# Transposes by DMA, permuted q/k weights, paired score rounds and a due-time order in a kernel of two attention and two FFN layers

## The chip, the cores and the metric

The kernel runs on one core of one Trainium2 chip. The metric is the device time of one execution in microseconds. The core's engines are TensorE (PE, with its weight loads as PEld), VectorE (DVE), ScalarE (ACT), GpSimd (POOL) and SyncE (SP, which here only issues DMAs). Each runs its own instruction list in order, and they meet at semaphores.

## The reference

x has 2048 tokens of 640 features. The program is x = x + A(LN(x)); x = x + B(LN(x)), done twice with the same weights. All inputs are bf16.

```python
def A(x):                     # 32 heads of 20, 4 segments of 512 tokens
    q, k, v = heads(x @ wq), heads(x @ wk), heads(x @ wv)
    M, z = 0, 0
    for s in range(4):
        p = softmax(q_s @ k_s.T * 20**-0.5 + causal_mask)
        a_dot = p @ v_s
        a_mem = (phi(q_s) @ M) / (phi(q_s) @ z + 1e-6)
        o_s = g * a_mem + (1 - g) * a_dot         # g = sigmoid(beta), per head
        M, z = M + phi(k_s).T @ v_s, z + phi(k_s).sum()
    return concat(o) @ wo
# phi(t) = t + 1 if t > 0 else exp(t)
def B(x): return relu(x @ w1) @ w2                # 640 -> 1728 -> 640
```

## The kernel before

The work goes by layer a (0, 1) and segment s (0 to 3) of 512 tokens, four tiles of 128 tokens each. The whole of x stays in SBUF as `x_sb`. Generators (streams) yield operations; the class `Sched` takes at each step the operation that can start earliest by planned durations, and among equals the one of the stream with the smaller priority number. It does so while the program is built: what comes out is a fixed list of instructions for each engine. The streams are, from the first priority on, `scores`, `apply`, `repack`, `memory`, `proj`, `ffn`, then the constants and the loads.

`proj` (per segment) normalises: `stats` takes mean and variance of each tile on DVE (L419, L421), `chain` computes 1/sqrt in nine small DVE operations for the four tiles together (L429 to L436), then each tile is scaled (L465), transposed by five TensorE matmuls against `ident` into a PSUM bank (L444) and copied out to `xnT` (L448 on DVE or L449 on ACT). Then k and q come feature-major in five chunks of 128 features, each from five matmuls of 512 columns (L497), and are copied to `stg`; V comes token-major, in halves of 320 columns (L516), into `v_aug`, which holds a 21st column of ones per head.

A head has 20 features, so the chunks of 128 cut heads in two. `repack` therefore moves k and q by DMAs on SP's queue (L547) from `stg` to `pad`, where four heads (a group) stand at partitions 0, 32, 64 and 96.

`scores` takes one item, that is one group g of one segment: four heads run in four row tiles of TensorE, in three rounds: key block 0 (512 columns), blocks 1 and 3 (384 + 128), block 2 (256) (L695). Each round fills PSUM tiles X and Y, from which ACT takes the exponential to `PT` (L702), and POOL masks the diagonal blocks (L709). `apply` multiplies `PT` by `v_aug` (40 matmuls of 21 columns, L730), and DVE divides, weights by 1 - g and, for s > 0, adds to what `memory` has written in `o_sb`.

`memory` makes phi(q) and multiplies by the block-diagonal `BD` (L588), writes the quotient to `o_sb` (L600), transposes k back to tokens on TensorE (L622), makes phi(k), and adds phi(k).T v to `M_sb` (L649 to L659). `o_sb` has two buffers, one for each parity of s; `memory` takes it only when the output projection of two segments before has read it.

`ffn` is one stream: `out_proj` (transposes of `o_sb` through L444, then ten matmuls of 320 columns per tile, L786, added to x at L764), the second normalisation, 70 matmuls of 512 columns (L807) with ReLU to `hT` (L813, L811), and 112 of 320 columns (L826), added to x. The next segment's `out_proj` starts after the last of these. PSUM has eight banks: four for X and Y, one for `apply`, and three (MISC) for all else.

## Time and profile before

| | |
|---|---|
| median of 3 runs | 796.89 us (796.12 to 797.0) |
| span of the profiled execution | 797.5 us |
| mean granted TensorE clock | 0.902 |
| busy: PE, DVE, ACT, POOL | 84%, 54%, 54%, 22% |
| HBM read, written | 10.33 MB, 2.62 MB |

An engine's busy time is the union of its instructions' intervals. The idle time before an instruction is given with the instruction that released it. Matmuls overlap, so the cost of one in a stream is read from the distance between starts or from a long run of them, and not from its own duration.

### The profile page before, as it was taken

How to read it: one execution, taken by the hardware profiler on the slowest of the kernel's cores; microseconds unless marked ns; L12 is line 12 of the kernel's file. 1: busy time of each engine (PE TensorE's matmuls, PEld its weight loads, DVE VectorE, ACT ScalarE, POOL GpSimd, SP SyncE). 2: the span in 40 equal slices, each digit the busy share in tenths (PEclk: the TensorE clock that was granted, in tenths of full speed). 3: DMA queues.
4: the chain of work that ended last, by engine and by line, in shares of the span. 5: the costliest groups of instructions: out<-in, count | busy, mean ns of one | idle time of the engine just before them, and what ended most of it. 6: DMA issues, size and time to landing. Idle time of an engine off the chain costs nothing.

```text
span 797.5 us, 16459 instructions
## 1 busy us (share of the span) xinstructions
PE 667.2 (84%) x6944; PEld 383.1 (48%) x6944; DVE 433.7 (54%) x1253; ACT 430.1 (54%) x593; POOL 172.3 (22%) x274
## 2 busy tenths in 40 slices
PE   0969579999987999889995899859998599579488
PEld 0435345546554455555463545635556346336335
DVE  4333769697378533783449745496453833611611
ACT  0467778887885686478821678216781175021030
POOL 3022333333332223122310233103330032000000
PEclk9969759999997999979997799967999699969889
DMA  8711100200110110002000020000200000000000
GB/s 283 261 42 32 37 1 9 46 16 2 41 28 1 36 33 2 1 8 46 18 1 1 6 47 17 1 1 10 46 14 35 1 1 18 18 0 25 9 0 34
DMA packets 22809, 24.50 MB, mean 31 GB/s; under 512 B 3472, under 2 KB 22096, under 8 KB 22736
## 3 DMA queue, kind: packets, MB, share of 16 engines
q1 hardware_dynamic: 22592, 23.44, 10.9%
q8 instruction: 54, 0.88, 0.4%
q14 instruction: 19, 0.16, 0.1%
q0 software_dynamic: 144, 0.02, 0.0%
HBM read 10.33 MB, written 2.62 MB: 16 GB/s over the span
## 4 chain that ended last, share of the span: by engine, by line
PE 73%; DVE 20%; ACT 4%; issue 1%; DMA 1%; POOLq 0%
PE ps L807 16%; PE ps L826 16%; PE ps L497 12%; PE ps L730 7%; PE ps L695 7%; PE ps L516 6%; DVE stats L419 5%; PE ps L786 4%; ACT PT L702 3%; PE ps L444 3%; DVE x_sb L764 3%; DVE xnT L448 2%; DVE xn_tok L465 2%; DVE o_sb L600 2%; PE ps L649 1%
## 5 line engine op out<-in xcount | busy, mean ns | idle before, releaser
L702 ACT ACTIVATE PT<-ps 128x1024 bf16<-128x1024 f32 (+1 forms) x384 | 317.5, 880 | 133.0 <-PE ps L695 131.9
L709 POOL TENSOR_SCALAR_AFFINE_SELECT PT<-PT 128x512 bf16<-128x512 bf16 x256 | 165.9, 660 | 492.2 <-ACT PT L702 492.1
L807 PE MATMUL ps<-xnT,w_r 128*128 128x512 bf16 x560 | 145.6, 391 | 2.2 <-DVE xnT L448 1.8
L764 DVE TENSOR_TENSOR x_sb<-x_sb,ps 128x320 bf16<-128x320 bf16 x128 | 61.9, 484 | 144.4 <-PE ps L826 128.1
L826 PE MATMUL ps<-w_r,hT 128*128 128x320 bf16 x896 | 131.4, 299 | 3.7 <-ACT hT L813 2.9
L826 PEld LDWEIGHTS ps<-w_r,hT 128*128 128x128 bf16 x896 | 84.5, 98 | 42.6 <-issue 5.9
L695 PE MATMUL ps<-pad 20*128 20x512 bf16 (+3 forms) x1024 | 75.3, 328 | 17.2 <-ACT PT L702 16.8
L813 ACT ACTIVATE hT<-ps 128x512 bf16<-128x512 f32 x62 | 37.1, 598 | 97.0 <-PE ps L807 96.6
L730 PEld LDWEIGHTS ps<-v_aug,PT 128*128 128x128 bf16 x2560 | 74.0, 98 | 23.3 <-issue 12.3
L730 PE MATMUL ps<-v_aug,PT 128*128 128x21 bf16 x2560 | 76.0, 174 | 9.6 <-DVE rstd L436 4.5
L444 PE MATMUL ps<-ident,xn_tok 128*128 128x128 bf16 x320 | 36.8, 262 | 56.2 <-DVE xn_tok L465 55.9
L807 PEld LDWEIGHTS ps<-xnT,w_r 128*128 128x128 bf16 x560 | 51.9, 100 | 60.6 <-issue 11.6
L786 PE MATMUL ps<-wo_r,oT 128*128 128x320 bf16 x320 | 53.2, 308 | 20.4 <-DVE oT L448 12.7
L497 PE MATMUL ps<-xnT,wk_r 128*128 128x512 bf16 x200 | 58.2, 407 | 1.0 <-DVE xnT L448 0.6
L695 PEld LDWEIGHTS ps<-pad 20*128 20x128 bf16 x1024 | 20.9, 93 | 78.0 <-ACT PT L702 43.0
L444 PEld LDWEIGHTS ps<-ident,xn_tok 128*128 128x128 bf16 x320 | 24.6, 116 | 70.2 <-DVE xn_tok L465 66.6
L497 PE MATMUL ps<-xnT,wq_r 128*128 128x512 bf16 x200 | 56.8, 396 | 0.0
L419 DVE BATCH_NORM_STATS2 stats<-x_sb 128x6 f32<-128x320 bf16 x128 | 55.6, 461 | 0.0
L516 PE MATMUL ps<-wv_r,xnT 128*128 128x320 bf16 x320 | 55.3, 300 | 0.2 <-DVE xnT L448 0.2
L811 DVE TENSOR_SCALAR hT<-ps 128x512 bf16<-128x512 f32 x50 | 34.4, 689 | 35.2 <-PE ps L807 34.8
L739 DVE RECIPROCAL rden<-ps 128x16 f32<-128x16 f32 x64 | 16.3, 255 | 60.9 <-PE ps L730 60.7
L786 PEld LDWEIGHTS ps<-wo_r,oT 128*128 128x128 bf16 x320 | 28.7, 99 | 35.9 <-DVE oT L448 16.0
(63 smaller groups left out, 578.5 us busy)
## 6 DMA issues: line engine op xcount, KB each, us to landing
pad<-stg SPq DMA_DIRECT2D x224, 40.0 KB
out_dram<-x_sb SPq DMA_DIRECT2D x16, 160.0 KB, 1.8
w_r<-in_B_w_dram SPq DMA_DIRECT2D x1, 2160.0 KB, 14.8
w_r<-in_B_w_dram SPq DMA_DIRECT2D x1, 2080.0 KB, 16.2
x_sb<-in_A_x_dram SPq DMA_DIRECT2D x3, 640.0 KB, 12.5
wk_r<-in_A_wk_dram SPq DMA_DIRECT2D x1, 800.0 KB, 9.1
wq_r<-in_A_wq_dram SPq DMA_DIRECT2D x1, 800.0 KB, 10.9
wv_r<-in_A_wv_dram SPq DMA_DIRECT2D x1, 800.0 KB, 12.6
```

Source lines behind the costliest of these rows:

```text
L419: tk = yield dve(320, 1, lambda e, c2=c2: e.bn_stats(stats6[:, t, c2, :], x_sb[:, t, c2 * 320:(c2 + 1) * 320]), xt)
L444: tk = yield pe(56.0 * FC, [(lambda e, c=c: e.transpose(pb[:, c * 128:(c + 1) * 128], srcs[c], ident[:]), c == FC - 1) for c in range(FC)] ...
L497: tk = yield pe(mm_ns(512), [(lambda e, k=k, w_r=w_r, c=c, bk=bk: e.matmul(bk.ap[:, :], w_r[:, k, c * 128:(c + 1) * 128], xt.ap[:, k, :], ...
L516: tk = yield pe(mm_ns(320), [(lambda e, k=k, i=i, hf=hf, bk=bk: e.matmul(bk.ap[:, 0:320], xt.ap[:, k, i * 128:(i + 1) * 128], wv_r[:, k, h ...
L695: fns.append((lambda e, j=j, hh=hh, N=N, o=o: e.matmul(ps[:, hh, o:o + N], sl.ap[32 * hh:32 * hh + DH, 0, 128 * j:128 * j + 128], sl.ap[32 ...
L702: tx = yield act(2 * w, lambda e, k=k, bkp=bkp, u=u, w=w: e.activation(pt.ap[:, 2 * k:2 * k + 2, PT_AT[u]:PT_AT[u] + w], bkp.ap[:, :, 0:w] ...
L709: tm = yield pool(600.0, lambda e, reg=reg: e.affine_select(out=reg, in_=reg, pattern=[[0, 4], [1, 128]], compare_op=ALU.is_ge, fill=0.0, ...
L730: fns.append((lambda e, i=i, hh=hh, j=j: e.matmul(od[:, i, hh, :], pt.ap[:, hh, PT_OFF[j] + 128 * (i - j):PT_OFF[j] + 128 * (i - j) + 128] ...
L764: ta = yield dve(320, 1, lambda e: e.tensor_tensor(x_sb[:, t, 320 * hf:320 * hf + 320], x_sb[:, t, 320 * hf:320 * hf + 320], bk.ap[:, 0:32 ...
L786: tk = yield pe(mm_ns(320), [(lambda e, k=k, hf=hf, bk=bk, ot=ot: e.matmul(bk.ap[:, 0:320], ot.ap[:, k, :], wo_r[:, k, hf * 320:(hf + 1) * ...
L807: tk = yield pe(mm_ns(512), [(lambda e, k=k, dc=dc, bk=bk: e.matmul(bk.ap[:, :], w1_r[:, k, dc * 128:(dc + 1) * 128], xt.ap[:, k, :], star ...
L826: tk = yield pe(mm_ns(320), [(lambda e, dc=dc, i=i, hf=hf, bk=bk: e.matmul(bk.ap[:, 0:320], hT[:, dc, i * 128:(i + 1) * 128], w2_r[:, dc, ...
```

## The change

The whole body is rewritten; the computation stays.

- The columns of wq and wk are copied on chip (`permute`) so that the five chunks hold groups 0 to 4 (heads 8r + g in row tile r) directly in `kqA`, in 20 of each 32 partitions. The other 12 hold pieces of groups 5 to 7, which `relay` writes to a DRAM scratch and reads back to `kqL`. `repack` is gone.
- All transposes (normalised tiles, attention output, keys) are DMA transposes issued by SP. The 1/sqrt is a power on POOL.
- Two items share their score rounds: five rounds of 512 columns per pair, the exponentials all 1024 wide.
- The weight 1 - g is put into the 21st column of `v_aug` and into `maskg`, so one small DVE operation per item goes.
- The order is by earliest start and then by a due time in units of segments; PE and ACT time that `scores` is about to use is kept free for it. The evacuations are streams of their own, and so are `o_turn`, `out_proj` and the two normalisations; `ffn` is due 1.4 to 2.4 segments after its own.
- Weights are loaded by ACT's and POOL's queues, x of segment 0 by SP in four DMAs.

```diff
+MODE_NS = 100.0
+
+HOT = 1.0
+
+RESERVE = ("scores",)
+TOL = 60.0
...
-                end, start, k = self._best(st[2])
-                key = (round(start), st[0], n)
+                b = self._best(st[2], None if st[5] in RESERVE else resv)
+                if b is None:
+                    continue
+                end, start, k, rank = b
+                key = (round(rank), st[2].due, n)
...
+def xbar(sem, tiles, fn, waits=(), acq=(), users=1):
+    return Op([("sp", 200.0 + 27.0 * tiles, 0.0, one(fn))], waits, acq, users, dma=(sem, 15.0 * tiles, 1700.0))
...
+        def loads_act():
+            yield from ld("act", "wv", 819200, lambda e: e.dma_start(wv_r[:], w_src(A_wv)), ("wv",))
+            yield from ld("act", "wk", 819200, lambda e: e.dma_start(raw[0], w_src(A_wk)), ("wkr",))
+            yield from ld("act", "wq", 819200, lambda e: e.dma_start(raw[1], w_src(A_wq)), ("wqr",))
...
+        def permute():
+            got = {0: [], 1: []}
+            for n, (wp, key) in enumerate(((wk_p, "wkr"), (wq_p, "wqr"))):
+                w = yield Need(key)
+                src = raw[n].rearrange("p k (r d) -> p k r d", r=4)
+                for c in range(FC):
+                    dst = wp[:, :, c * 128:(c + 1) * 128].rearrange("p k (r d) -> p k r d", r=4)
+                    for d0, d1, s0 in ((0, 20, 20 * c), (20, 32, 100 + 12 * c)):
+                        o, i = dst[:, :, :, d0:d1], src[:, :, :, s0:s0 + d1 - d0]
+                        tk = yield evac(20 * (d1 - d0), 2, lambda e, o=o, i=i: e.tensor_copy(o, i),
+                                        lambda e, o=o, i=i: e.activation(o, i, ACT.Copy), w, psum=False)
+                        got[n].append(tk)
+                    S.set(("wk", "wq")[n], c, v=got[n][-2:])
+            HT[0].drop(*(got[0] + got[1]))
...
-            tch = yield from chain(4 * s, 4, aggr)
+                tu = yield pool(200, lambda e, sl=sl: e.tensor_scalar(
+                    lnU[:, sl], mv[:, sl, 1], LN_EPS, None, ALU.add), aggr)
+                tr = yield pool(500, lambda e, sl=sl, n=n: e.tensor_tensor(
+                    rstd[:, sl], lnU[:, sl], nhalf[:, 0:n], ALU.pow), [tu] + nh)
...
-                tT, tc = yield from transposes([bx.ap[:, c * 128:(c + 1) * 128] for c in range(FC)], [tn],
-                                               xt.ap[:, :, i * 128:(i + 1) * 128], xt.tks, idt)
+        def dma_x(i, bx, waits, slot):
+            k = slot.ap
+            return xbar(xnt_sem[k][i], 40, lambda e, k=k, i=i, bx=bx: e.dma_start_transpose(
+                xnT[:, k, i, :, :], bx.ap), waits)
...
-        def repack(a, s):
+        def relay(a, s):
+            b = s % 2
+            ev = []
+            for c in range(5):
+                r = yield Need("kq", a, s, c)
+                ev += r
+            wr = []
+            sc = None
+            for r in range(4):
+                f = lambda e, r=r: e.dma_start(
+                    scr[b, r].rearrange("(q j) f -> j q f", j=12),
+                    kqA[32 * r + DH:32 * r + 32, b].rearrange("p n c f -> p (n c) f"))
+                if sc is None:
+                    tk, sc = yield dma("sp", scw_sem[b][r], 122880, lambda e, s_, f=f: f(e), ev, [SCR[b]])
+                else:
+                    tk = yield dma("sp", scw_sem[b][r], 122880, f, ev + sc.old)
+                wr.append(tk)
+            for c in range(5):
+                KQA[b][c].drop(*wr)
+            rd = []
+            sl = None
+            for r in range(4):
+                f = lambda e, r=r: e.dma_start(
+                    kqL[32 * r:32 * r + DH].rearrange("p n m f -> p (n m) f"),
+                    scr[b, r].rearrange("(q d) f -> d q f", d=DH))
+                if sl is None:
+                    tk, sl = yield dma("sp", scr_sem[r], 122880, lambda e, s_, f=f: f(e), [wr[r]], [KQL],
+                                       users=3 + (s > 0) + (s < NSEG - 1))
+                else:
+                    tk = yield dma("sp", scr_sem[r], 122880, f, [wr[r]] + sl.old)
+                rd.append(tk)
+            sc.drop(*rd)
...
+                n0 = 4 if h == 0 else 1
+                tk, kt = yield xbar(ktk_sem[0], 32 * n0, lambda e, d, h=h, n0=n0: e.dma_start_transpose(
+                    d[:, 0:n0].rearrange("p g i t -> p (g i) t"),
+                    kqA[:, b, 0, 4 * h:4 * h + n0].rearrange("p g f -> p (g f)")), ev, [KTK])
+                for c in range(4 * h, 4 * h + n0):
+                    KQA[b][c].drop(tk)
+                tks = [tk]
+                if h == 1:
+                    ev = yield Need("kqL", a, s)
+                    tk = yield xbar(ktk_sem[1], 96, lambda e, d=kt.ap: e.dma_start_transpose(
+                        d[:, 1:4].rearrange("p g i t -> p (g i) t"), kqL[:, 0].rearrange("p g f -> p (g f)")), ev + kt.old)
+                    KQL[0].drop(tk)
+                    tks.append(tk)
+                ph = []
+                for g0, g1 in ((0, 2), (2, 4)):
+                    w = g1 - g0
+                    blk = ktok[:, g0:g1].rearrange("p g i t -> p (g i t)")
+                    te, et = yield act(512 * w, lambda e, d, blk=blk: e.activation(d, blk, ACT.Exp), tks, [ET], psum=False)
+                    tm = yield dve(512 * w, 4, lambda e, blk=blk: e.tensor_scalar(
+                        blk, blk, 0.0, 1.0, ALU.max, ALU.add), [te])
+                    tp = yield dve(512 * w, 2, lambda e, blk=blk, d=et.ap: e.tensor_tensor(blk, blk, d, ALU.min), [tm, te])
...
-        ROUNDS = ((0,), (1, 3), (2,))
-        PT_W = (512, 512, 256)
+            rounds = (((0, 0, 0),), ((0, 1, 0), (0, 3, 384)), ((0, 2, 0), (1, 2, 256)),
+                      ((1, 0, 0),), ((1, 1, 0), (1, 3, 384)))
...
+        def o_turn(a, s):
+            ow = []
+            for g in range(G):
+                r = yield Need("o", (a * NSEG + s) * G + g)
+                ow += r
+            ob = yield Need("ob", a, s)
+            tks = []
+            for i in range(NJ):
+                tk, ot = yield XT(i, ob, ow)
+                tks.append(tk)
+                S.set("oT", a, s, i, v=[ot, tk])
+            ob.drop(*tks)
...
-        S.add(5, each(ffn))
+        S.add(paced(scores, 32, lambda m: (m / 4 - 9, (m + 1) / 4 - 9, 30)), "scores")
+        S.add(paced(apply, 64, lambda m: (m / 8 - 8.9, m / 8 - 8.7, 8)), "apply")
+        each(ln1, "ln1", -1.0, -0.8, 24)
+        each(proj_kq, "kq", -0.8, -0.3, 60)
+        each(relay, "relay", -0.4, -0.3, 8)
+        each(proj_v, "v", -0.8, -0.2, 48)
+        each(mem_write, "mwrite", -0.2, 0.5, 30)
+        each(mem_read, "mread", -0.2, 0.5, 50)
+        each(o_turn, "oturn", -1.0, -0.9, 4)
+        each(out_proj, "oproj", -0.9, -0.8, 48)
+        each(ln2, "ln2", -1.0, -0.8, 24)
+        each(ffn, "ffn", 1.4, 2.4, 220)
```

## Rows read from the trace of the kernel before

**Rows 1.** Engine totals on the page: busy us, share of the span, instructions.
```profile
PE 667.2 (84%) x6944; PEld 383.1 (48%) x6944; DVE 433.7 (54%) x1253; ACT 430.1 (54%) x593; POOL 172.3 (22%) x274
```

**Rows 2.** Stretches: length, busy PE, PEld, DVE, ACT, POOL; clock, DMA share, GB/s.
```profile
120.00:220.00 100.00, 96.66 (x1201) 54.99 (x1201) 71.33 (x200) 82.86 (x115) 34.48 (x52) 1.00 0.11 23
...
420.00:440.00 20.00, 11.67 (x128) 7.15 (x128) 18.36 (x75) 2.49 (x5) 0.00 (x0) 0.75 0.00 1
...
675.00:797.50 122.50, 91.98 (x581) 54.49 (x577) 39.52 (x106) 16.72 (x28) 0.00 (x0) 0.89 0.04 14
```

**Rows 3.** The longest wait of TensorE: total us, times, longest us.
```profile
PE ps L444 <- DVE xn_tok L465: 55.9, 30, 16.7
```

**Rows 4.** Timeline from 676 us on: start, us, engine, line, operation, idle before.
```profile
692.14 0.88 DVE L419 BATCH_NORM_STATS2 stats<-x_sb 128x6 f32<-128x320 bf16 x2
...
698.58 0.71 PE L444 MATMUL ps<-ident,xn_tok 128*128 128x128 bf16 x5 [6.88 <-DVE xn_tok L465]
...
704.84 17.79 PE L807 MATMUL ps<-xnT,w_r 128*128 128x512 bf16 x70 [0.59 <-DVE xnT L448]
```

**Rows 5.** Timeline at the boundary near 420 us.
```profile
421.73 0.45 PE L444 MATMUL ps<-ident,o_sb 128*128 128x128 bf16 x5
...
425.37 0.34 PE L588 MATMUL ps<-BD,stg 128*128 128x147 bf16 x3
```

**Rows 6.** Runs at full clock in the chain, and a weight load in the timeline.
```profile
269.04 1.08 PE ps L497 x5
...
298.13 1.00 PE ps L730 x40
...
779.17 15.40 PE ps L826 x112
...
422.08 0.28 PEld L444 LDWEIGHTS ps<-ident,xn_tok 128*128 128x128 bf16 x5
```

**Rows 7.** Groups of TensorE instructions from 280 to 320 us: busy us, mean ns.
```profile
L807 PE MATMUL ps<-xnT,w_r 128*128 128x512 bf16 x68 | 17.0, 380 | 0.0
L826 PE MATMUL ps<-w_r,hT 128*128 128x320 bf16 x77 | 11.6, 300 | 0.0
L730 PE MATMUL ps<-v_aug,PT 128*128 128x21 bf16 x200 | 5.8, 172 | 0.0
L516 PE MATMUL ps<-wv_r,xnT 128*128 128x320 bf16 x30 | 5.4, 300 | 0.0
L695 PE MATMUL ps<-pad 20*128 20x512 bf16 (+3 forms) x80 | 5.4, 302 | 0.0
```

**Rows 8.** The exponentials, all together and those of 1024 columns.
```profile
L702 ACT ACTIVATE PT<-ps 128x1024 bf16<-128x1024 f32 (+1 forms) x384 | 317.5, 880 | 133.0 <-PE ps L695 131.9
...
L702 ACT ACTIVATE PT<-ps 128x1024 bf16<-128x1024 f32 x256 | 248.1, 1022 | 95.9 <-PE ps L695 95.1
```

**Rows 9.** The three groups of transposes on TensorE, whole span.
```profile
L444 PE MATMUL ps<-ident,xn_tok 128*128 128x128 bf16 x320 | 36.8, 262 | 56.2 <-DVE xn_tok L465 55.9
...
L444 PE MATMUL ps<-ident,o_sb 128*128 128x128 bf16 x160 | 14.8, 225 | 0.4 <-DVE xnT L448 0.3
...
L622 PE MATMUL ps<-ident,stg 128*128 128x128 bf16 x120 | 14.2, 271 | 1.2 <-DVE o_sb L600 0.8 <-ACT phk L630 0.2 <-DVE oT L448 0.2
```

**Rows 10.** SP's packing DMAs by instruction, and landing times (us) of others.
```profile
L547 SPq DMA_DIRECT2D pad<-stg x288: 641/768/1397, 28.1 to 582.0; - x144
...
out_dram<-x_sb SPq DMA_DIRECT2D x16, 160.0 KB, 1.8
...
x_sb<-in_A_x_dram SPq DMA_DIRECT2D x2, 320.0 KB, 3.7
```

**Rows 11.** Timeline of the start: first statistics, first projection, first score round.
```profile
9.64 0.88 DVE L419 BATCH_NORM_STATS2 stats<-x_sb 128x6 f32<-128x320 bf16 x2
...
22.98 2.31 PE L497 MATMUL ps<-xnT,wk_r 128*128 128x512 bf16 x5 [0.59 <-DVE xnT L448]
...
46.21 0.61 PE L695 MATMUL ps<-pad 20*128 20x512 bf16 x4
```

More of the change, by code (lines that the diff above doesn't have):

```diff
@@ L124, in __init__, with take, drop @@
         self.tks = []
[L126 to L134 removed]
+        self.left = 0
+    def take(self, users=1):
+        assert self.free, self.name
+        self.free = False
+        self.left = users
+        self.old = self.tks
+        self.tks = []
+        return self
+    def drop(self, *tks):
+        assert not self.free, self.name
+        self.tks = self.tks + [t for t in tks if t is not None]
+        self.left -= 1
+        if self.left == 0:
+            self.free = True
+class Op:
+    def __init__(self, alts, waits, acq=(), users=1, mode="full", dma=None, early=0.0, hold=()):
+        self.alts = alts
+        self.waits = [t for t in waits if t is not None]
+        self.acq = acq
+        self.hold = hold
+        self.users = users
+        self.mode = mode
+        self.dma = dma
+        self.due = -1.0
+        self.early = early
 class Need:
@@ new lines, in ld, with w_src, loads_sp @@
+        def ld(e, name, nbytes, fn, key, waits=(), issue=700.0):
+            tk = yield dma(e, sem_("d_" + name), nbytes, fn, waits, issue=issue, rate=250.0)
+            S.set(*key, v=[tk])
+            return tk
+        xs = A_x[0].rearrange("(t p) d -> p t d", p=128)
+        def w_src(w):
+            return w.rearrange("(c p) d -> p c d", p=128)
+        def loads_sp():
+            for i in range(4):
+                yield from ld("sp", "x0%d" % i, 163840, lambda e, i=i: e.dma_start(x_sb[:, i, :], xs[:, i, :]), ("x", 0, i))
@@ L837, in ffn @@
-            HT.release(tk)
-            S.set("xB", b, s, tks=res)
-        dout = sem_("d_out")
-        AS = [(a, s) for a in range(2) for s in range(NSEG)]
-        def each(f):
-            for a, s in AS:
-                yield from f(a, s)
-        def items(f):
-            for n in range(2 * NSEG * G):
-                yield from f(n)
-        S.add(0, items(scores))
-        S.add(1, items(apply))
-        S.add(2, each(repack))
-        S.add(3, each(memory))
-        S.add(4, each(proj))
```

1206 lines of the change are left out of this document (665 added, 541 removed).

## The prediction

> **What bounds the kernel now.** I read the engine totals first [rows 1]. TensorE is busy 667.2 of 797.5 us, DVE and ACT about 430 each, POOL 172. No engine is full, so the end is set by TensorE's work plus the stretches in which it waits or runs at the lower clock. Which of the two weighs more is read from the busy time by stretch [rows 2]. From 120 to 220 us TensorE is busy 96.66 of 100 us at a granted clock of 1.00 (2.4 GHz), while DVE is at 71 and ACT at 83: so the three engines can run side by side with hardly a gap. From 420 to 440 it is busy 11.67 of 20 at a clock of 0.75, ACT works 2.49 us of the 20 and DVE 18.36. From 675 to the end, 122.5 us, it is busy 91.98.
>
> The waits of TensorE name the gap: 55.9 us on the normalised tokens [rows 3]. The timeline of the last segments shows its form [rows 4]: the statistics start at 692.14, the first transposes come at 698.58 after 6.88 us idle, and the FFN's first matmul only at 704.84, because tile after tile goes DVE, TensorE, DVE. In the middle it is worse, since `ffn` is one serial stream that also contains `out_proj`: the transposes of the attention output run at 421.73, and only then may `memory` write that `o_sb` buffer again, its first matmul coming at 425.37 [rows 5]; `apply` waits for that, keeps the tile of probabilities, and the exponentials stop.
>
> **The floor of TensorE before.** Prices at the full clock [rows 6]: 1.08 us for five 512-column matmuls (0.216), 15.40 for 112 of 320 columns (0.1375), 1.00 for the 40 of one `apply`, 0.28 for five weight loads of 128 columns (0.056). The score rounds are the remainder of a full stretch, 280 to 320 us [rows 7]: 68 x 0.216 + 77 x 0.1375 + 200 x 0.025 + 30 x 0.1375 = 34.4 of 40 us, so 5.6 us for 80 score matmuls. An item has 16 of them in three rounds, so these are 15 rounds at 0.373 us, against 427 columns on average, which alone take 0.178. About 0.195 us of a round is therefore fixed.
> The program has 960 matmuls of 512 columns (207.4 us), 1536 of 320 (211.2), 64 applies (64.0), 192 rounds (71.6), 264 memory matmuls (15) and 600 transposes (34). Sum 604. So some 194 of the 797.5 us are waits, the ramp and the lower clock.
>
> **The change, part by part.**
> *Transposes to the crossbar.* All 600 leave TensorE: 65.8 us of busy time [rows 9], but at full clock 600 x 0.056 = 34 us, and only that is certain. Their PSUM evacuations go too; DVE and ACT are not the bound, so I count nothing for them.
> *Score rounds.* Five rounds of 512 columns for two items instead of six: 160 x (0.213 + 0.195) = 65.3 us, 6.3 less. On ACT 320 exponentials of 1024 columns at 248.1 / 256 = 0.969 us are 310 us [rows 8] where there were 317.5: a small gain on an engine with room.
> *Memory matmuls.* 192 reads and 192 writes of 84 columns instead of 264, at the weight load's 0.056: 22 us, 7 more. The padded heads make the phi work 8/5 as wide on ACT and DVE; both have room.
> *Sum:* 207.4 + 211.2 + 64 + 65.3 + 22 = 570 us, 34 below the old floor.
> *Normalisation.* The nine small DVE operations become two on POOL, and the transposes no longer bind DVE to TensorE. `o_turn` and `out_proj` are streams of their own, so the o_sb buffer comes free without waiting for the FFN of the segment before, and the FFN of one segment lies beside the scores of the next one or two. That cover is why I count the stall of the boundaries as mostly gone. If it is not there, 55.9 us of waits [rows 3] and their low clock stay.
> *SP's queue.* 288 packing DMAs at a median of 0.768 us [rows 10] go. In come 114 transposes (96 of 128x640, 18 of key blocks), together 672 blocks of 128x128, and 64 relay DMAs. The trace has no transpose by DMA. Its lower bound is the cost of an ordinary instruction here, 114 x 0.768 = 88 us. The upper is a block that costs as much as the slowest packing DMA, 672 x 1.397 = 939 us. The relay adds 64 x 0.768 = 49. I take a value near the lower end, since one instruction carries five to sixteen blocks: 150 to 250 us of SP, hidden. What waits behind a late one is the whole queue: the next normalisation, the relay and the output's turn.
> *Relay.* A write to DRAM and a read back, each 1.8 to 3.7 us to land [rows 10], plus eight issues of 0.768: 10 to 13.5 us until groups 5 to 7 of a segment can be scored. Groups 0 to 3 cover it with two pairs of ten exponentials, 19 us. Without that cover 8 x 13.5 = 108 us would be at stake; with it, nothing.
> *Start.* The first projection matmul now comes at 22.98 us and the first score round at 46.21 [rows 11]. Loading V first, normalising tile by tile and scoring groups 0 to 4 without packing should bring the first projections to about 15: the tiles' statistics begin at 9.64, then one tile's chain and a landing of 1.8 to 3.7. The permuting copies are bounded by 0 and 20 x 1.022 (the 1024-column exponential, the longest ACT row here) = 20 us on two engines; four of them precede the first pair, so 0 to 4 us; I take 1, inside the 15.
> *End.* The last group of matmuls ends at 779.17 + 15.40 = 794.57 [rows 6], the span at 797.5: 3 us, kept.
>
> A rule that speaks against the change: the round trip through TensorE costs a tile (704.84 - 698.58) / 4 = 1.57 us of DVE and TensorE in turns [rows 4]. The Trainium skill, "VectorE: DVE Perf Modes", section "The three transpose paths", gives 390 ns for a 128x128 transpose on TensorE and 1309 ns for the crossbar, and advises TensorE where PSUM as destination is fine. At 1.309 us a block, one after the other, SP's transposes alone would be 880 us. No row here shows the crossbar. In this trace TensorE's own price is the 0.056 us spacing, far under the page's figure for one alone, so the crossbar's may be a latency too.
>
> **The time.** 570 us at the fill of the best stretch (96.66%) are 590; plus 15 before and 3 after, 608. The boundaries will not vanish: I leave two us at each of the seven between segments, 14 us. The forecast is 622. The profiled span (797.5) and the median of the runs (796.89) differ by 0.1%, so no correction is made. With all full it would be 570 + 15 + 3 = 588, the lower end. The engines leave room: ACT at about its 430 us and DVE at less than its 434 are under 70% of 622, below the 83 and 71 of the full stretch.
>
> **The rivals.**
> *Late landings (faster, but less).* The order of each engine is fixed ahead from planned durations, a transpose being planned at 1.28 us of SP and 1.7 us of landing after that. If the chip takes longer, each engine waits in order. There are 24 turns (two normalisations and one output per segment, eight segments). At 3 us each that is 72 us, 694; at worst the boundaries stay as they are: 797.5 - 34 - 8 (the start) = 755. For it: nothing in the trace tests the plan's figure, and DVE, ACT and SP are all in strict order. Against: the full stretch shows that a planned order holds at 97%, and the FFN lags by over one segment, which gives slack. 670 to 755.
> *SP becomes the bound (slower).* SP executes every transpose and relay in order. With 49 us for the relay it passes 797 us when a block of 128x128 occupies it for (797 - 49) / 672 = 1.11 us. The slowest packing DMA is above that (1.397: 988 us), the median below (0.768: 565 us). At the figure of the Trainium skill above, 1.309, it would be 929 us. Against it: an instruction is issued per 5 to 16 blocks, so even the slowest row per instruction gives 114 x 1.397 = 159 us. I place it midway between 797 and 988, at 890.
> *The change does not do what it says.* The FFN stays in step with the scores (one hT buffer, three spare PSUM banks), so that only the removed work is gained: 797.5 - 34 = 763 us.
>
> **How the numbers follow.** Forecast (588 to 670): 0.61. Late landings (670 to 755): 0.22. Removed work only (755 to 790): 0.04. Nothing measurable: 0.02. SP the bound or another slow queue (over 800): 0.11. The predicted time is the likeliest case, 622. The range of 8 in 10 takes in the forecast's case and most of the late landings: 588 to 745. A run of this kernel tells apart about 0.2% from no change; faster by more than that: 0.87, within it 0.02, slower 0.11.
>
> **What would show it.** Right: TensorE's busy time between 575 and 625 us; no stretch of 20 us in the middle under 17 busy and the clock near 1.0 there; the wait on normalised tokens gone from the list of waits and nothing over 15 us in its place; the first projection matmul before 18 us; SP's transposes of 128x640 at about 1 to 2 us each and queued behind nothing; ACT working right through a segment's boundary. Wrong: TensorE waiting for the transposed tiles (then it is the late landings, and the landing times tell by how much), SP issuing back to back through the whole span (then it is the bound), ACT again silent for 20 us at the boundaries (then the coupling has stayed), or rounds of more than 0.41 us.

## The result, and the profile after

| | median of 4 runs | span of the profiled run | TensorE busy | mean granted clock |
|---|---|---|---|---|
| before (beside it) | 796.94 us | 797.5 us | 667.2 us (84%) | 0.902 |
| after | 651.21 us | 646.8 us (time 649.16) | 587.2 us (91%) | 0.966 |

The change makes the kernel faster: the ratio is 0.8163, 95% interval 0.8126 to 0.8199. The forecast was 622 (588 to 745), so the sign and the case were right and the time came out 29 us above it. Of all runs told of below one was slow: one of the six of a_rounds6 took 941.95 us at a granted clock of 0.566, and its ratio is of the other five, whose median is 649.13.

The engine totals of the page of after, which answer to [rows 1] (busy us, share of the span, instructions):

```profile
PE 587.2 (91%) x6464; PEld 336.0 (52%) x6464; DVE 406.5 (63%) x1014; ACT 410.6 (63%) x488; POOL 197.9 (31%) x316
```

TensorE lost 80 us of busy time, more than the 34 of work at full clock. The transposes alone had been busy for 65.8 us [rows 9], and the mean granted clock has risen from 0.902 to 0.966; how the rest divides between the two isn't worked out here. The stretches of after, which answer to [rows 2] (length, then busy PE, PEld, DVE, ACT, POOL; granted clock, DMA share, GB/s):

```profile
0.00:40.00 40.00, 17.21 (x84) 8.07 (x84) 24.63 (x72) 13.62 (x26) 13.00 (x27) 0.91 0.76 192
...
60.00:140.00 80.00, 62.73 (x776) 34.65 (x774) 57.80 (x154) 55.66 (x61) 29.80 (x46) 0.83 0.54 105
140.00:594.00 454.00, 445.13 (x5141) 257.77 (x5140) 299.85 (x736) 316.09 (x367) 145.58 (x229) 1.00 0.30 49
594.00:646.80 52.80, 42.57 (x254) 24.81 (x252) 12.52 (x31) 8.36 (x14) 1.27 (x2) 0.94 0.16 38
...
420.00:440.00 20.00, 19.25 (x208) 9.71 (x201) 14.29 (x29) 14.68 (x18) 6.12 (x11) 1.00 0.20 34
```

From 140 to 594 us TensorE is busy 445.13 of 454 us. The stretch 420 to 440, where it was busy 11.67 us and ACT 2.49 [rows 2], has 19.25 and 14.68. What is left lies in three stretches: 0 to 40, 60 to 140 and from 594 on.

To put a number on each stretch I price its matmuls at the full clock, with the prices of the prediction, and call the rest of its length *lost*, be it a wait or a lower clock. From 60 to 140 us, for example, the groups have 85 matmuls of 512 columns (18.4), 95 of 320 (13.1), 360 of `apply` (9.0), 96 of the memory (5.4) and nine rounds of 512, nine of 384 with 128 and eight halves of 256 (9.0): 54.9 of 80 us, so 25 are lost. Some 17 of them are idle (80 - 62.73), 8 are work at the clock of 0.83.

| stretch of after | 0–40 | 40–60 | 60–140 | 140–594 | 594–646.8 | sum |
|---|---|---|---|---|---|---|
| lost, us | 26.1 | 0.2 | 25.2 | 11.6 | 12.4 | 75.5 |
| **stretch of before** | **0–46** | | **46–120** | **120–681** | **681–797.5** | |
| lost, us | 27.5 | | 29.1 | 98.2 | 39.3 | 194.1 |

The 151 us between the two spans are 119 of lost time and 32 of work (603 to 571). Nearly all of the lost time that went is in the middle and at the end; the first 140 us gained next to nothing.

The waits of TensorE in after (total us, times, longest us), in place of [rows 3]:

```profile
PE ps L684 <- DMA xnT<-xn_tok: 21.6, 2, 14.6
PE ps L965 <- POOL PT L905: 9.1, 4, 3.4
PE ps L1088 <- DMA xnT<-xn_tok: 6.6, 1, 6.6
...
PE ps L1040 <- DMA oT<-o_sb: 2.6, 2, 2.3
```

The 55.9 us on the normalised tokens are gone, and 30.8 us on transposes by DMA have come (21.6 + 6.6 + 2.6). Of these, 28.2 are three waits, two at the start and one at the end; the other 2.6 lie in the middle. The wait of 14.6 is counted from the kernel's start, so 6.45 of it passed before the transpose was issued (the 55.9 held such a first wait too, of 16.7). The timeline of after at the start, against [rows 11] (start, us, engine, line, operation, idle before):

```profile
3.88 0.43 DVE L565 BATCH_NORM_STATS2 stats<-x_sb 128x6 f32<-128x320 bf16 x1
...
6.45 1.76 SPq L604 DMA_TRANSPOSE xnT<-xn_tok  x1
9.86 0.23 ACT L531 ACTIVATE gt<-beta_bc 128x32 f32<-128x32 f32 x1 [6.13 <-DMA beta_bc<-in_A_beta_dram]
10.12 0.18 DVE L532 TENSOR_SCALAR gt<-gt 128x32 f32<-128x32 f32 x1 [3.70 <-ACT gt L531]
...
14.59 2.85 PE L684 MATMUL ps<-wv_r,xnT 128*128 128x320 bf16 x10 [14.59 <-DMA xnT<-xn_tok]
...
24.47 4.41 PE L684 MATMUL ps<-wv_r,xnT 128*128 128x320 bf16 x20 [7.03 <-DMA xnT<-xn_tok]
...
28.71 1.24 PE L650 MATMUL ps<-xnT,wk_p 128*128 128x512 bf16 x5
```

The first tile's statistics begin at 3.88, where they began at 9.64 before [rows 11]. Its transpose is issued at 6.45 and TensorE starts on it at 14.59, 8.1 us later. DVE stands for 3.70 us behind the row of beta, so the second tile's statistics are late too. The timeline of after at the end, against [rows 4]:

```profile
606.55 0.45 DVE L578 TENSOR_SCALAR xn_tok<-x_sb,mv,rstd 128x640 bf16<-128x640 bf16 x1 [1.66 <-DMA xnT<-xn_tok]
...
607.88 1.21 SPq L592 DMA_TRANSPOSE xnT<-xn_tok  x1
...
610.59 17.28 PE L1088 MATMUL ps<-xnT,w_r 128*128 128x512 bf16 x70 [6.57 <-DMA xnT<-xn_tok]
...
628.56 15.39 PE L1108 MATMUL ps<-w_r,hT 128*128 128x320 bf16 x112 [0.69 <-ACT hT L1072]
```

The landing counts twice here. The fourth tile is normalised only at 606.55, since `xn_tok` has three buffers and the first comes free when its transpose has landed (1.66 us of waiting); its own transpose, issued at 607.88, lands 2.6 us later, and only then do the 70 matmuls start.

The transposes themselves, by line: duration of the issue on SP in ns (min/median/max), and below each, landing in us (min/median/max). First the tiles transposed one by one, then the other normalised tiles, then the attention output:

```profile
L604 SPq DMA_TRANSPOSE xnT<-xn_tok x16: 1199/1202/1938, 6.5 to 603.3; - x16
...
DMA to landing us min/median/max: 2.6/3.4/8.1
```
```profile
L592 SPq DMA_TRANSPOSE xnT<-xn_tok x48: 1199/1275/3462, 15.5 to 607.9; - x48
...
DMA to landing us min/median/max: 2.6/2.7/9.0
```
```profile
L1030 SPq DMA_TRANSPOSE oT<-o_sb x32: 1199/1252/3304, 108.9 to 593.7; - x32
...
DMA to landing us min/median/max: 2.5/2.7/6.8
```

One of five blocks occupies SP for 1.2 to 1.3 us in the median and lands in 2.7 (3.4 for the tiles transposed one by one), and in 7 to 9 at worst. The page "VectorE: DVE Perf Modes" of the Trainium skill, section "The three transpose paths", gives 1.309 us for a 128x128 block on the crossbar; by estimate that is 6.5 us for five, one after the other. The measured row of 2.7 us for five decides here.

### The profile page after: what moved, and what is told of

Same layout as the page of the kernel before. It is cut to its first block, busy times and chain, and to the rows that moved or that the text cites. A ratio compares the mean times of both kernels' runs of the same rounds, so it can differ in the third digit from the quotient of the medians.

```text
span 646.8 us, 15129 instructions
## 1 busy us (share of the span) xinstructions
PE 587.2 (91%) x6464; PEld 336.0 (52%) x6464; DVE 406.5 (63%) x1014; ACT 410.6 (63%) x488; POOL 197.9 (31%) x316
## 4 chain that ended last, share of the span: by engine, by line
PE 67%; DVE 13%; DMA 9%; ACT 5%; POOL 3%; issue 2%; SPq 0%; POOLq 0%
PE ps L1088 18%; PE ps L1108 15%; PE ps L650 9%; PE ps L965 8%; PE ps L916 7%; PE ps L1040 5%; PE ps L684 4%; ACT PT L936 3%; DMA xnT<-xn_tok 3%; DMA w_r<-in_B_w_dram 2%; DVE x_sb L1003 2%; DMA oT<-o_sb 2%; DVE stats L566 2%; DVE stats L565 2%; DVE xn_tok L578 1%
## 5 line engine op out<-in xcount | busy, mean ns | idle before, releaser
L936 ACT ACTIVATE PT<-ps 128x1024 bf16<-128x1024 f32 x256 | 248.2, 1023 | 110.6 <-PE ps L916 110.3
L684 PE MATMUL ps<-wv_r,xnT 128*128 128x320 bf16 x320 | 76.9, 321 | 22.9 <-DMA xnT<-xn_tok 21.6
L932 ACT ACTIVATE PT<-ps 128x1024 bf16<-128x1024 f32 x64 | 62.0, 1023 | 13.9 <-PE ps L916 13.9
L1071 DVE TENSOR_SCALAR hT<-ps 128x512 bf16<-128x512 f32 x65 | 44.9, 691 | 38.1 <-PE ps L1088 37.5
L650 PE MATMUL ps<-xnT,wk_p 128*128 128x512 bf16 x200 | 64.1, 389 | 1.8 <-DVE kqA L637 0.8
L1072 ACT ACTIVATE hT<-ps 128x512 bf16<-128x512 f32 x47 | 28.1, 598 | 57.3 <-PE ps L1088 56.8
L650 PE MATMUL ps<-xnT,wq_p 128*128 128x512 bf16 x200 | 62.0, 390 | 1.8 <-DVE v_aug L672 0.9
L684 PEld LDWEIGHTS ps<-wv_r,xnT 128*128 128x128 bf16 x320 | 32.0, 104 | 51.5 <-DMA xnT<-xn_tok 22.2
L578 DVE TENSOR_SCALAR xn_tok<-x_sb,mv,rstd 128x640 bf16<-128x640 bf16 x64 | 30.6, 490 | 28.6 <-DMA xnT<-xn_tok 18.1
L637 DVE CAST kqA<-ps 128x512 bf16<-128x512 f32 x54 | 36.8, 684 | 17.2 <-PE ps L650 17.0
L916 PE MATMUL ps<-kqA 20*128 20x512 bf16 (+3 forms) x640 | 41.1, 307 | 0.5 <-ACT PT L936 0.3
L1040 PEld LDWEIGHTS ps<-wo_r,oT 128*128 128x128 bf16 x320 | 29.1, 99 | 21.9 <-issue 4.8
```

The costliest lines, as they stand in the source:

```text
L650: fn = lambda e, bank, k=k, w_p=w_p, c=c: e.matmul(bank, w_p[:, k, c * 128:(c + 1) * 128], xnT[:, k_, :, k, :], start=(k == 0), stop=(k == ...
L684: fn = lambda e, bank, k=k, i=i, hf=hf: e.matmul(bank[:, 0:320], xnT[:, k_, i, k, :], wv_r[:, k, hf * 320:(hf + 1) * 320], start=(k == 0), ...
L916: fns.append((lambda e, x=x, j=j, hh=hh, N=N, o=o: e.matmul(ps[:, hh, o:o + N], kq(b, gg[x], 0)[32 * hh:32 * hh + DH, 128 * j:128 * j + 12 ...
L932: fn = lambda e, k=k, bp=bs.ap: e.activation(PT[:, :, 2 * k:2 * k + 2, 1024:1280], bp.rearrange("p h (x t) -> p x h t", x=2), ACT.Exp, sca ...
L936: fn = lambda e, k=k, bp=bs.ap, x=items[0], c0=c0: e.activation(PT[:, x, 2 * k:2 * k + 2, c0:c0 + 512], bp, ACT.Exp, scale=SCALE)
L1040: fn = lambda e, bank, k=k, hf=hf, o=ot.ap: e.matmul(bank[:, 0:320], o[:, k, :], wo_r[:, k, hf * 320:(hf + 1) * 320], start=(k == 0), stop ...
```

## The experiments

My theory of the gain, from the prediction: the coupling of the turn (attention output, output projection, second normalisation) to the serial FFN stream starved TensorE at each boundary, so most of the gain should come from separating them, and a smaller part from the removed TensorE work. The rival: the transposes and their evacuations were the cause, and the crossbar is the gain. Names with b_ are edits of the kernel before, names with a_ edits of the one after. Each run has its own runs of the kernel before beside it (796.8 to 798.0 us); the ratio is to these.

| kernel | median, us | ratio, 95% interval |
|---|---|---|
| b_oproj: before, `out_proj` a stream of its own | 774.58 | 0.9703 [0.9672, 0.9733] |
| b_oproj_ln2: and the second normalisation | 697.5 | 0.8749 [0.8731, 0.8767] |
| a_coupled: after, turn held | 660.15 | 0.8271 [0.8244, 0.8297] |
| a_nodue: after, fixed priorities | 658.86 | 0.8270 [0.8257, 0.8283] |
| a_nodue_coupled: both | 749.76 | 0.9408 [0.9381, 0.9436] |
| a_pe: after, 480 transposes on TensorE | 657.1 | 0.8237 [0.8221, 0.8252] |
| a_rounds6: after, six rounds | 650.06 | 0.8152 [0.8123, 0.8182] |
| a_first: after, first segment's on TensorE | 636.64 | 0.7990 [0.7967, 0.8013] |
| a_pool: after, GpSimd loads paced | 642.49 | 0.8047 [0.8033, 0.8061] |
| a_best2: a_first, a_pool, beta's landing | 656.58 | 0.8216 [0.8168, 0.8263] |
| a_best: and the last segment's | 653.01 | 0.8169 [0.8134, 0.8205] |
| a_first_last: first and last segment's on TensorE | 631.75 | 0.7920 [0.7900, 0.7940] |

**The streams alone, in the kernel before.**

```diff
+        def oproj(a, s):
+            xa = yield from out_proj(a, s)
+            S.set("xA", a, s, tks=xa)
         def ffn(b, s):
-            xa = yield from out_proj(b, s)
+            xa = yield Need("xA", b, s)
...
-        S.add(5, each(ffn))
...
+        S.add(5, each(oproj))
+        S.add(6, each(ffn))
...
```

> The kernel before, with one thing of the change alone: the output projection is a stream of its own, ahead of the feed-forward stream, instead of the first step of the feed-forward generator. Transposes, packing DMAs, streams' fixed priorities and rounds stay as they were. Theory A (the turn of the segment is what starved TensorE): the gaps at the five inner boundaries, where TensorE lost 20.8 to 22.2 us each by its work against the stretch's length, shrink to under 10 us, and the time falls from 797 to 700 to 740 us. Rival B (the loss came from the evacuations of the transposes and the packing DMAs that stay in): the boundaries lose as much as before and the time is 785 to 800 us.

Measured 774.58, 22.6 us less, which is between the ranges of the two theories. TensorE's wait on the normalised tokens hasn't changed (waits of b_oproj):

```profile
PE ps L444 <- DVE xn_tok L465: 58.2, 31, 14.9
```

So the half of the turn that I had not separated holds the larger part. The next kernel gives the second normalisation a stream as well (`ln2`, between `oproj` and `ffn`, in the same way).

> As b_oproj, and the second normalisation is a stream of its own too, ahead of the feed-forward matmuls. Theory A: it takes most of what is left at the boundaries, 665 to 710 us, at least 10 us below b_oproj. Rival B: no lower than b_oproj; 785 to 800 us. Where A holds, what is left against the changed kernel (651) is TensorE work taken away (33 us by my sum) and the start.

Measured 697.5. The same wait is halved (waits of b_oproj_ln2):

```profile
PE ps L444 <- DVE xn_tok L465: 27.0, 16, 14.9
```

Two streams, with every transpose still on TensorE and the packing as it was, bring 99.7 of the 146 us. The rival falls as the main cause. The 77.1 us of the second step are worth that much once the output projection is apart; the second normalisation as the only separate stream was not run.

**The turn held, in the kernel after.**

```diff
         def o_turn(a, s):
+            k = a * NSEG + s - 1
+            if k >= 0:
+                yield Need("xB", k // NSEG, k % NSEG, NJ - 1, 1)
```

> The changed kernel, with the attention output of a segment held back until the feed-forward of the segment before has been stored, which is the order that the kernel before had; everything else (crossbar transposes, permuted weights, shared rounds, due times) as in the changed kernel. Theory A (the decoupled turn is the larger part of the gain): the stalls at the boundaries come back, about five times 15 to 20 us: 720 to 760 us. Rival B (the removed TensorE work and the crossbar are the gain): under 670 us.

Measured 660.15: 9 us. My theory, in the form that I had given it, fell, and the time lies in the rival's range (under 670); the two b_ kernels above and a_pe below speak against the rival's reason. The turn follows the FFN of the segment before again, and the boundaries stay full. What else differs is the order among the streams: the kernel before ran the FFN last of all, the one after runs each step by its due time. The next two runs take the due times away: `PRIO` gives each kind of step a fixed rank, the scores first and the FFN behind all other matmuls.

```diff
-                key = (round(rank), st[2].due, n)
+                key = (round(rank), PRIO[st[5]], n)
```

> The changed kernel with a fixed priority for each kind of step (rounds, then apply, relays, memory, first normalisation and projections, output turn and second normalisation, feed-forward last) instead of due times; streams, crossbar and shared rounds stay. Of the 146 us that the change brings, 100 came back to the kernel before by making the output projection and the second normalisation streams of their own (697.5 against 797.2), so the streams are settled and this run asks for the order among them. Theory A (streams alone suffice; due times are worth little): 648 to 668 us. Rival B (the due times carry a large part of the 46 us between 697.5 and 651): 680 us or more.

> As a_nodue, and the attention output of a segment is held back until the feed-forward of the segment before has been stored, as in a_coupled, which cost only 9 us (660.2 against 651.2) where I had expected 70 to 110. Theory A (that hold was cheap because the due-time order keeps other work back as cover; with fixed priorities the feed-forward runs last and nothing is left to cover the turn): 700 to 760 us, at least 40 us above a_nodue. Rival B (the hold is cheap because the second normalisation is a stream of its own): within 20 us of a_nodue.

Together the four kernels make a table (median us):

| | turn free | turn held |
|---|---|---|
| due times | 651.2 | 660.2 |
| fixed priorities | 658.9 | 749.8 |

a_nodue is inside theory A, too. With either one in place the kernel is within 9 us of the one with both; taking both away costs 98.6 us. Theory A of a_nodue_coupled holds. The stretches of the two held kernels show how; first with due times, then with fixed priorities (columns as above):

```profile
460.00:480.00 20.00, 19.77 (x254) 13.11 (x247) 17.66 (x50) 15.28 (x17) 6.32 (x11) 1.00 0.37 69
480.00:500.00 20.00, 19.88 (x253) 11.63 (x251) 16.23 (x42) 14.59 (x17) 7.03 (x11) 1.00 0.33 52
```
```profile
460.00:480.00 20.00, 19.31 (x125) 11.97 (x124) 5.69 (x14) 6.07 (x9) 0.00 (x0) 1.00 0.00 1
480.00:500.00 20.00, 16.75 (x195) 10.10 (x194) 17.67 (x55) 10.24 (x13) 5.62 (x8) 0.83 0.43 76
```

With fixed priorities the FFN runs in one block once nothing else can; POOL does nothing from 460 to 480, and what follows has no FFN beside it. ACT's timeline of that kernel (a_nodue_coupled) shows the block:

```profile
468.06 1.05 ACT L832 ACTIVATE phq<-kqA 128x1024 bf16<-128x1024 bf16 x1
488.26 1.94 ACT L939 ACTIVATE PT<-ps 128x1024 bf16<-128x1024 f32 x2 [19.14 <-PE ps L919]
```

ScalarE does nothing for 19.14 us, much as at the boundary of the kernel before (2.49 us busy of 20 [rows 2]). As these rows read, TensorE pays for it outside the block, where no FFN fills its gaps: from 430 to 530 us it is busy 81.36 of 100 us, and its longest waits are on the exponentials (5.7 and 3.8 us) and the masks (4.2), not on the turn's transposes (1.2). With due times, where FFN matmuls are spread between the rounds, it is busy 98.48 us between the same times, with 1.1 us of waits on exponentials.

**The crossbar.** The edit gives both normalisations and the attention output five TensorE transposes per tile and an evacuation by VectorE or ScalarE, in place of the transpose by DMA; the key transposes stay.

```diff
+        def pe_t(srcs, waits):
+            idt = yield Need("ident")
+            tT, bk = yield pe(56.0 * FC, lambda bank: [(lambda e, c=c: e.transpose(
...
+                if True:
+                    tT, bk, src = yield from pe_t([ob.ap[:, i, c * 128:(c + 1) * 128] for c in range(FC)], ow)
...
+                    continue
                 tk, ot = yield XT(i, ob, ow)
```

> The changed kernel with the transposes of both normalisations and of the attention output on TensorE again (480 of them, each group of five evacuated by VectorE or ScalarE); the key transposes stay on the crossbar. Theory A (the crossbar only saves the TensorE time of the transposes): 480 x 0.056 = 27 us of TensorE work come back and the wait for the first transposed rows (14.6 and 7.0 us) shrinks: 660 to 680 us. Rival B (the crossbar is the source of the gain by freeing evacuations and banks): 710 us or more. Rival C (the landing of the crossbar's transposes costs what it saves): 640 to 655 us.

Measured 657.1, 5.9 above after, which is between A and C. By the same accounting a_pe has 598.2 us of work, 27 more, and 58.7 lost, 17 less: 18.4 to 40 us, 20.7 from 60 to 140, 14.5 from 140 to 594, 4.8 at the end. Its totals and its longest wait:

```profile
PE 619.4 (94%) x6944; PEld 363.0 (55%) x6944; DVE 423.8 (65%) x1075; ACT 430.3 (66%) x523; POOL 197.7 (30%) x318
...
PE ps L627 <- DVE xn_tok L584: 13.7, 8, 6.6
```

So the crossbar takes 27 us of work off TensorE and gives 17 back as lost time: 7.7 before 40 us and 7.6 from 594 us on, where TensorE waits for landings, and 4.5 from 60 to 140, less 2.9 in the middle. The two profiled spans differ by these 10 us (656.9 to 646.8). DVE and ACT carry the evacuations with room to spare.

**Shared rounds.**

```diff
-            rounds = (((0, 0, 0),), ((0, 1, 0), (0, 3, 384)), ((0, 2, 0), (1, 2, 256)),
-                      ((1, 0, 0),), ((1, 1, 0), (1, 3, 384)))
+            rounds = (((0, 0, 0),), ((0, 1, 0), (0, 3, 384)), ((0, 2, 0),),
+                      ((1, 0, 0),), ((1, 1, 0), (1, 3, 384)), ((1, 2, 0),))
...
```

> The changed kernel with six rounds for a pair of items again: the last 256 columns of each item in a round of their own, with one exponential of 512 columns per partition for each. The exponentials take what they took before (317.5 against 310.2 us, +7 us on ScalarE), and TensorE starts 64 more rounds of 256 columns in place of 64 halves of a shared one: +6.3 us by my sum. Theory A (TensorE's sum sets the time): 653 to 661 us. Rival B (the rounds are covered): within 2 us of 651. Rival C (shorter rounds hand the banks back earlier and the masks need not wait for a shared round): 1 to 6 us faster than 651.

Measured 650.06, its interval overlapping that of after: no difference. TensorE is busy 594.1 us, 6.9 more, as priced, and the span is the same (647.4). The 6.3 us that I had subtracted for the rounds are not there in the time; since TensorE is the bound only from 140 to 594 us, I would have expected some of it. By the same accounting this kernel loses 22.4 us from 60 to 140 and 10.1 from 594 on, 2.8 and 2.3 less than after; why it does I haven't shown.

**The start.** `pe_t` as above, for the first segment's normalisation alone (`if single:`).

> The changed kernel with the first segment's normalised tokens alone (twenty of the 128x128 blocks for each item) transposed on TensorE and evacuated, the rest on the crossbar. In the changed kernel TensorE waits 14.6 us for the first transposed tile, which lands 8.1 us after its issue, and 7.0 us for a second. Theory A (the late landing is the start's loss): the first projection starts some 4 to 8 us earlier and the time falls by 6 to 14 us, to 637 to 645. Rival B (the loads and the beta row bound the start, and the landing only hides it): 648 to 653 us.

Measured 636.64, 14.6 us under after: theory A, a little past the end of its range (637 to 645). TensorE's timeline of a_first:

```profile
6.65 0.71 PE L627 MATMUL ps<-ident,xn_tok 128*128 128x128 bf16 x5 [6.65 <-DVE xn_tok L584]
7.95 2.85 PE L711 MATMUL ps<-wv_r,xnT 128*128 128x320 bf16 x10 [0.59 <-DVE xnT L589]
14.24 0.71 PE L627 MATMUL ps<-ident,xn_tok 128*128 128x128 bf16 x5 [3.44 <-DVE xn_tok L584]
...
23.77 1.25 PE L677 MATMUL ps<-xnT,wk_p 128*128 128x512 bf16 x5 [0.58 <-DVE xnT L589]
```

From the end of the normalisation to the first projection it takes 1.3 us where it took 8.1, and the first key projection starts at 23.77 instead of 28.71. The loss to 40 us falls from 26.1 to 18.5 and that from 60 to 140 from 25.2 to 21.1.

**GpSimd's loads.** In the stretch of 60 to 140 us the timeline of after shows a load that GpSimd issues only when the one before it has landed, and masks behind it:

```profile
64.33 0.79 POOL L493 DMA_DIRECT2D w_r<-in_B_w_dram  x1 [4.88 <-DMA w_r<-in_B_w_dram]
65.13 1.82 POOL L905 TENSOR_SCALAR_AFFINE_SELECT PT<-PT 128x512 bf16<-128x512 bf16 x3
...
65.84 1.24 PE L965 MATMUL ps<-v_aug,PT 128*128 128x21 bf16 x40 [3.37 <-POOL PT L905]
...
68.09 1.94 ACT L936 ACTIVATE PT<-ps 128x1024 bf16<-128x1024 f32 x2 [3.79 <-PE ps L916]
```

```diff
+                if s > 1:
+                    w = []
+                    yield Need("p", s - 1, 3)
...
+                yield Need("p", 3 + k // 2, 3)
+                w = []
                 tk = yield dma("pool", sem_("d_w1%d" % k), 442368, lambda e, k=k: e.dma_start(
...
```

> The changed kernel, in which GpSimd's weight and x loads are issued after given mask steps instead of each when the load before it has landed (there GpSimd, which works in order, waits up to 4.88 us for a landing with masks behind it, and TensorE then waits 3.37 us for the masked tile). Between 60 and 140 us TensorE lost 25 us by its work against the length. Theory A (those landings behind which masks queue are the main cause): TensorE's wait for masked tiles (9.1 us) falls under 3 us, the loss between 60 and 140 us falls by 5 to 15 us, and the time to 636 to 646 us. Rival B (the stretch is short of TensorE work that may run, and the masks only end the wait): 647 to 655 us.

Measured 642.49, 8.7 us under after, and yet not for the reason given. TensorE's wait for masked tiles did fall from 9.1 to 3.3 us, but the loss from 60 to 140 us is 28.3, not smaller than 25.2; what fell is above all the loss up to 40 us, from 26.1 to 20.9. A stretch of after, then those of a_pool:

```profile
20.00:40.00 20.00, 14.36 (x74) 6.72 (x74) 12.12 (x34) 7.95 (x12) 6.51 (x11) 0.83 0.71 171
```
```profile
20.00:40.00 20.00, 20.00 (x132) 9.71 (x130) 9.88 (x23) 11.86 (x18) 5.83 (x9) 1.00 0.48 85
40.00:60.00 20.00, 19.60 (x234) 10.77 (x231) 15.28 (x36) 17.49 (x23) 8.74 (x13) 1.00 0.67 167
60.00:80.00 20.00, 9.27 (x124) 5.22 (x122) 10.57 (x30) 11.93 (x13) 7.68 (x12) 0.64 0.95 164
```

The loads have moved out of the first 40 us, where they ran beside the first transposes: the DMA share from 20 to 40 us is 0.48 in place of 0.71, and TensorE's second wait for a transposed tile is 2.96 us in place of 7.03. They have come into 60 to 80, where the DMA share is 0.95 and TensorE waits 6.3 us for a transposed tile. The time got better, the theory of masks did not.

**Put together.** a_best2 joins a_first, a_pool and `lat=6500.0` for the row of beta in the plan; a_best adds the last segment's transposes on TensorE.

> a_first (636.6) and a_pool together, and the planner is given 6.5 us for the landing of the beta row. If both gains add: 622 to 634 us. If the stretch of 60 to 140 us is short of work whatever GpSimd does: 634 to 640 us.

> As a_best2, with the second normalisation and the attention output of the very last segment transposed on TensorE too. In the changed kernel TensorE waits 6.6 us at the end for a transposed tile, and lost 12.4 us from 594 us on by its work against the length; with all transposes on TensorE that stretch lost 4.8 us. Theory A (the end is bound by the landing): 5 to 9 us below a_best2. Rival B (the end is bound by the chain of normalisation and store, whatever transposes): within 2 us of a_best2.

Measured 656.58 and 653.01: both gains are gone, 20 and 16 us above a_first, and a_best2 is outside both of its ranges. a_best is 3.6 us below a_best2, between its two theories and with overlapping intervals, so the times don't decide on the end. Its losses do: from 594 us on a_best loses 4.4 us, a_best2 10.5. The loss from 60 to 140 us is 26.5 in a_best2 and 35.8 in a_best (21.1 in a_first), and the chain of waits of a_best has one piece of it:

```profile
71.22 20.95 DMA ktok<-kqA
```

A transpose of key blocks, issued at 71.22, lands 20.95 us later, beside the paced weight loads; ScalarE works in order and stands behind it (waits of a_best from 60 to 110 us):

```profile
ACT etmp L801 <- DMA ktok<-kqA: 17.6, 1, 17.6
...
PE ps L685 <- DMA xnT<-xn_tok: 14.9, 1, 14.9
```

Pacing and beta's figure came in together, so which of them set this order can't be said; a_first with a_pool alone was not tried. The last run leaves GpSimd's loads and beta as in after.

> a_first (636.6) with the attention output and the second normalisation of the very last segment on TensorE too; the loads of GpSimd as in the changed kernel, since in a_best they met the key transposes, one of which landed 20.95 us after its issue with ScalarE queued behind it. In a_best, whose end has the same edit, TensorE lost 4.4 us from 594 us on against 10.5 in a_best2. Theory A (the two ends of the kernel are independent of each other and of the middle): 636.6 less 5 to 7 us: 629 to 633 us. Rival B (late landings in the first 140 us vary with any change of the plan and eat it): 634 to 650 us.

Measured 631.75, 4.9 us under a_first: A, at its edge. It is 3% below the changed kernel by the ratios (0.7920 to 0.8163), and the end shows why (timeline of a_first_last):

```profile
594.35 0.44 PE L627 MATMUL ps<-ident,xn_tok 128*128 128x128 bf16 x5
594.63 1.11 PE L1143 MATMUL ps<-w_r,hT 128*128 128x320 bf16 x7
595.58 15.27 PE L1123 MATMUL ps<-xnT,w_r 128*128 128x512 bf16 x70
```

The transposes lie between matmuls of the FFN before, and the last 70 start without a wait, at full clock (15.27 against 17.28 us).

## Why the prediction was right, and where it was off

- **The floor.** Forecast 570, by the trace 571; the old one 604 against 603. The 571 are the trace's matmuls at the forecast's own prices, so they test the counts. The prices are borne out from 140 to 594 us, where they give 442.4 us of work and TensorE is busy 445.13. That the 34 us come off the time is not borne out: a_pe brings back 27 of them and costs 5.9, a_rounds6 brings back 6.3 and costs nothing.
- **The boundaries.** Forecast: mostly gone, 14 us left. In the 454 us after 140 TensorE lost 11.6 in all. The prediction named the separate turn and the FFN beside later scores as one cover. The table of four shows two, the free turn and the due times, of which either suffices. Within the turn, the second normalisation (77 us, separated second) weighs more than the output projection (22.6, separated first), which I had put first by [rows 5].
- **The fill and the boundaries together** were 34 us (20 + 14); measured 37 (0.2 + 25.2 + 11.6), of which 25 lie between 60 and 140 us, a ramp that the sum doesn't have. I took the fill of the best stretch for the whole kernel; that the two sums are close is luck, since the middle lost far less than the 34 and the ramp made up for it.
- **The start.** Forecast 15, lost 26. The step that failed is "a landing of 1.8 to 3.7": those are the landings of ordinary DMAs [rows 10], and the first transposes landed 8.1 to 9.0 us after their issue at a DMA share of 0.76. The first projection did come near 15 us, at 14.59, but by two errors that cancel: the statistics began at 3.88 and not at 9.64, and the landing took 8.1. What the sum left out is the next landing, for which TensorE waited another 7.03 us; the first key projection moved from 22.98 to 28.71. a_first takes the transposes of this term away and gains 14.6 us; TensorE's losses fall by 7.6 us before 40 us and by 4.1 between 60 and 140.
- **The end.** Forecast 3, lost 12.4. I kept the 3 us behind the last matmul and left out that the last turn has no cover: its transposes land 2.6 us or more after their issue, the fourth tile waits for the first one's buffer besides, and TensorE stands for 6.57. a_first_last against a_first: 4.9 us.
- **The sum.** 1 (floor) + 11 (start) + 9 (end) + 3 (fill and boundaries) + 2.4 (from the span to the time) = 26 us, against 649.16 - 622 = 27 of the profiled run (the terms are rounded).
- **Late landings.** As a rival it was priced at each of 24 turns. In the changed kernel it shows at the two ends (28.2 us of waits, 6.45 of them before the first issue), and the middle hides the landings of 2.7 us behind other work but for 2.6 us of waits. So the rival's mechanism was at work, at two turns and not at 24. a_best shows it at full size in one place, 20.95 us.
- **The relay.** Counted at nothing, hidden by the pairs of groups 0 to 3. No engine has a wait on the relayed tiles (`kqL`) in the list of after: as said.
- **SP.** 1.2 us for an instruction of five blocks, nearer to the price by instruction (0.768) than to that by block (five of 1.397). By the medians of its rows that is, as an estimate, 147 us for the 114 transposes and 23 for the 64 relay DMAs, inside the 150 to 250 of the forecast. SP isn't the bound: it waits for others most of all (49.1 us in one place, for the sums that it stores).
- **Signs named ahead.** TensorE busy 587 (575 to 625), no 20 us from 140 to 580 under 17 busy (the least is 17.67, at 300 to 320), ACT at work at the boundary, and no wait over 15 us in place of the old one (14.6 at most): as said. By total, as [rows 3] counts, the wait on transposed tiles is 21.6 for the first projections and 30.8 in all, and TensorE waiting for transposed tiles was named as a sign of late landings: that sign came at the two ends. A round's matmuls are busy 0.39 to 0.40 us. By the distance between starts, with what is lost just before it, it takes about 0.41, the price and the limit named (timeline of after; from start to start 0.63, less 0.216 for the matmul):

```profile
425.98 0.38 PE L650 MATMUL ps<-xnT,wk_p 128*128 128x512 bf16 x1
426.29 0.39 PE L916 MATMUL ps<-kqL 20*128 20x512 bf16 x4
426.61 0.31 PE L684 MATMUL ps<-wv_r,xnT 128*128 128x320 bf16 x1
```

- **Open.** What makes the loss of 25.2 us from 60 to 140 us isn't shown: a_pool took most of the waits on masks away and the loss stayed. From b_oproj_ln2 (697.5) to a_nodue (658.9), both with fixed priorities and a free turn, are 38.6 us, of which a_pe and a_rounds6 account for about 6. The rest lies with what else the change has: the query and key packing (permuted weights, no padding DMAs, no key transposes on TensorE), the order of the first loads, the evacuations as streams of their own, the time kept free for `scores`, the power on GpSimd and the folded weight 1 - g; no run took them apart.

## What to carry to other kernels

When one engine is the bound and still waits, look first at which steps share a serial stream: here making two of them streams of their own, with fixed priorities, was worth 100 us. In the changed kernel the separate turn and the due times covered for each other: one of the two was enough, and without both 99 us were lost. A transfer that replaces engine work is free only where other work covers its landing, so the first and the last turn, which have no cover, were better left on the engine here. Two edits that each gained alone, one by moving transposes and one by moving loads, gained nothing together with a third small change of the plan, and the loads met a transpose elsewhere; a joint run belongs to every sum of gains.

## What the runs showed of the hardware that was not expected

- The landing of a transpose of five blocks varied with the other traffic: 2.6 to 3.2 us for the last four, with a DMA share of 0.16 from 594 us on, and 8.1 to 9.0 beside the first loads, with a share of 0.76. A transpose of key blocks landed after 20.95 us in a_best, with a share of 0.97 from 60 to 80 us, where the twelve of after that read `kqA` took 2.4 to 7.7. a_pool, which moves loads away, shortens the second wait at the start (2.96 for 7.03 us); that the traffic alone sets the landing isn't isolated.
- The power on GpSimd for 128x4 values takes 1.04 us, and 0.58 for 128x1 (timeline of after, the first in the last normalisation's path at 601.75, the second in the first's):

```profile
5.36 0.58 POOL L574 TENSOR_TENSOR rstd<-lnU,nhalf 128x1 f32<-128x1 f32 x1
...
601.75 1.04 POOL L574 TENSOR_TENSOR rstd<-lnU,nhalf 128x4 f32<-128x4 f32 x1
```

- Gaps are paid twice. From 60 to 140 us, with 17 us idle in pieces, the mean granted clock is 0.83, and by the accounting above 8 of the 25 lost us are work done slower; in a_first_last the last FFN, with no gap ahead of it, takes 15.27 us where after took 17.28.
